# Sigmoid attention and a gated FFN on one core: batch 0 cut into 256 and 192 queries, its loads and FFN runs rearranged, and the first down tile one burst later

## The chip, the cores and the metric

The kernel runs on one core of one Trainium2 chip. The time is the device time of one execution in microseconds (us); medians are over several executions. The profile is of one execution, and its span is some 1.8 us shorter than the device time (429.5 us against 431.3 us for the profiled execution of the kernel before). A program on one core has no second die to compare with, so an execution counts as slow when it is over 1.5% above the fastest of its kernel.

## The reference, cut to what matters

```python
def _attn_ref(q, k, v):                       # (8 batches, 12 heads, 448, 64)
    scores = scale * np.matmul(q, k.transpose(0, 1, 3, 2)) - np.log(S)
    attn = 1.0 / (1.0 + np.exp(-scores))      # a sigmoid: no sum over keys
    return np.matmul(attn, v)

def _moe_ref(x, w_gate, w_val, w_out):        # x: 3584 x 768, hidden 1536
    gate = np.maximum(x @ w_gate, 0.0)
    return (gate * (x @ w_val)) @ w_out
```

Heads of one batch are put side by side to give x. As the attention has no sum over keys, a part of the queries can go all the way through it alone.

## The kernel before

TensorE does five things: scores (`qk_ps`, 64x64 tiles), the product with the values (`pv_ps`, "PV"), a gate and a value product for one of twelve chunks of the hidden layer (`g_ps`, `v_ps`, a "pair"), a down tile (`ya` and `yb`, from the hidden layer with the output weights `wo`), and, for batches 0 and 1, transposes (`trt`). ScalarE does the sigmoids and most rectifiers. VectorE copies transposes, scales PV into xT and multiplies gate and value. GpSimd issues the loads, each of which casts to fp16.

Batch 0 starts from nothing, so it is cut by queries into two halves and runs in six slots (three groups of four heads for each half). A slot has four units: scores, then one sigmoid over up to two chunks of keys. The dictionary `after` says what TensorE is given after each unit. Dummy matmuls (`keep_warm`) fill time.

```python
    QCUT = 3                                  # 3 x 64 = 192 queries first, then 256
    HALVES = ((0, QCUT), (QCUT, NCH))
    ...
    load_gv(0, 2)                             # gate and value weights, chunks 0 and 1
    load(0, 1, NG, "q", QCUT)                 # the rest of batch 0's queries
    load_gv(2, 4)
    load_gv(4, 6)
    load(1, 0, 1, "kq")
    load_gv(6, 9)
    load(1, 1, 2, "kq")
    load_gv(9, 12)
    load_v(1)                                 # the values of batch 1
    load(1, 2, 3, "kq")
    ...
    after = {
        ...                                   # transposes and dummies of the first half
        (3, 0): slots[0].pv,
        (3, 1): two_pv,                       # slots 1 and 2
        (3, 2): lambda: ffn_mix("f"),         # one pair
        (3, 3): second_queries,               # a pair, then transposes
        (4, 1): slots[3].pv,
        (4, 2): lambda: ffn_mix("f"),
        (4, 3): lambda: ffn_mix("f"),
        (5, 1): slots[4].pv,
        (5, 2): lambda: ffn_mix("f"),
        (5, 3): lambda: ffn_mix("f"),
    }
    ...
    def late_loads():                         # near the end of batch 1
        dma_transposes(2, 1)
        hold(2, 1)                            # GpSimd waits here for that transpose
        load_v(2)
        load_o()                              # the output weights wo
    ...
        elif b == 2:                          # "y" is a down tile
            mix = ["ff", "ff", "ffy", "ff", "ffy", "ffy"]
```

From batch 1 on, each batch is six bursts of scores and PVs, each followed by a run of pairs and down tiles of the batch before.

## Time and profile before

| | kernel before |
|---|---|
| device time, median | 431.05 us (430.83 to 431.26, 3 runs) |
| span of the profile | 429.5 us |
| TensorE busy | 418.5 us (97%) |
| ScalarE, VectorE busy | 201.1 us (47%), 141.8 us (33%) |
| TensorE's waits for wo | 1.9 and 1.2 us, at the first down tile |
| loads, 7 to 50 us | about 200 GB/s without a pause |

Read this table from the second row to the last. When one engine is busy 97% of the time, little is gained from making another faster (a stretch in which it only runs dummies counts as busy too, and may be bound by another engine), and what can go is the 3% of holes and any work that is not needed (the dummies). So the holes have to be found one by one, and for each one the question is what ended it.

### The profile page before, as it was taken

To read this page: it belongs to the slowest core of one execution; us is meant where nothing else is said; L and a number is where in the kernel's file an instruction comes from. 1 tells how busy PE (TensorE), PEld (TensorE's weight loads), DVE (VectorE), ACT (ScalarE), POOL (GpSimd) and SP (SyncE) were. 2 spreads that over 40 slices of the span, in tenths; PEclk is the share of its full clock that TensorE was granted. 3 is DMA by queue.
4 is the path that set the end of the run, shared out by engine and by line. 5 is a ranking of instruction groups with operands and counts; after the bars stand their busy time and mean duration, and the time that the engine had idled before them with its cause. 6 is when DMAs were issued, how large, how long until landed. Compare 5 with 4: busy or idle time off the path is not lost.

```text
span 429.5 us, 8576 instructions
## 1 busy us (share of the span) xinstructions
PE 418.5 (97%) x3668; PEld 231.9 (54%) x3668; DVE 141.8 (33%) x277; ACT 201.1 (47%) x424; POOL 49.8 (12%) x73
## 2 busy tenths in 40 slices
PE   8899999889999999999999999999999999999996
PEld 3677774345555455545545455545545554555563
DVE  2453443224233243233242243332442322322231
ACT  5766787434444454446443743473473446122000
POOL 9543204400030001200030000100000000000000
PEclk9999999999999999999999999999999999999999
DMA  9999958999799033951389114721243101100134
GB/s 147 198 202 203 203 81 131 203 220 195 110 155 182 0 81 82 169 104 38 85 122 182 46 43 82 127 56 38 44 88 75 37 2 38 37 2 0 46 102 110
DMA packets 68789, 43.63 MB, mean 102 GB/s; under 512 B 35600, under 2 KB 65168, under 8 KB 68752
## 3 DMA queue, kind: packets, MB, share of 16 engines
q0 software_dynamic: 30736, 23.37, 36.5%
q1 hardware_dynamic: 37664, 19.47, 22.7%
q8 instruction: 28, 0.46, 0.4%
q10 hardware_dynamic: 352, 0.26, 0.2%
q14 instruction: 9, 0.07, 0.1%
HBM read 47.19 MB, written 11.01 MB: 136 GB/s over the span
## 4 chain that ended last, share of the span: by engine, by line
PE 78%; DMA 13%; issue 5%; POOL 3%; DVE 0%; ACT 0%; POOLq 0%
PE g_ps L297 21%; PE v_ps L297 21%; PE ya L335 16%; PE yb L335 9%; PE qk_ps L222 6%; PE pv_ps L240 5%; DMA wo<-in_moe_w_out_dram 4%; DMA v<-in_v_dram 4%; DMA q<-in_q_dram 3%; DMA wg<-in_moe_w_gate_dram 2%; POOL k L97 1%; POOL q L97 1%; POOL v L103 1%; POOL v L101 0%; DVE xT L168 0%
## 5 line engine op out<-in xcount | busy, mean ns | idle before, releaser
L177 ACT ACTIVATE PT<-qk_ps 128x448 f16<-128x448 f32 (+3 forms) x318 | 151.6, 584 | 123.2 <-PE qk_ps L222 122.3
L297 PE MATMUL g_ps<-xT,wg 128*128 128x448 f16 (+2 forms) x648 | 127.5, 333 | 0.2 <-DVE xT L168 0.2
L297 PE MATMUL v_ps<-xT,wv 128*128 128x448 f16 (+2 forms) x648 | 126.8, 332 | 0.3 <-DMA wv<-in_moe_w_val_dram 0.3
L315 DVE TENSOR_TENSOR hT<-gate_sb,v_ps 128x448 f16<-128x448 f32 (+2 forms) x108 | 61.0, 569 | 164.5 <-PE v_ps L297 98.0
L335 PEld LDWEIGHTS <-hT 128*128 128x128 f16 x672 | 65.6, 98 | 50.6 <-DMA wo<-in_moe_w_out_dram 4.0
L297 PEld LDWEIGHTS <-wg 128*128 128x128 f16 x648 | 58.4, 98 | 56.5 <-issue 15.8
L297 PEld LDWEIGHTS <-wv 128*128 128x128 f16 x648 | 62.3, 98 | 47.9 <-DMA wv<-in_moe_w_val_dram 0.6
L306 ACT ACTIVATE gate_sb<-g_ps 128x448 f32<-128x448 f32 (+2 forms) x102 | 54.4, 544 | 70.8 <-PE g_ps L297 70.6
L335 PE MATMUL ya<-wo,hT 128*128 128x512 f16 x336 | 77.1, 379 | 1.9 <-DMA wo<-in_moe_w_out_dram 1.9
L222 PE MATMUL qk_ps<-qkT 64*64 64x448 f16 (+2 forms) x756 | 48.0, 336 | 1.9 <-ACT PT L177 1.1
L335 PE MATMUL yb<-wo,hT 128*128 128x256 f16 x336 | 41.3, 273 | 1.2 <-DMA wo<-in_moe_w_out_dram 1.2
L168 DVE TENSOR_SCALAR xT<-pv_ps 128x448 f16<-128x448 f32 (+2 forms) x54 | 28.4, 568 | 30.8 <-PE pv_ps L240 30.8
L343 DVE TENSOR_SCALAR ysb<-ya 128x512 f32<-128x512 f32 x28 | 19.4, 692 | 56.9 <-PE ya L335 55.0
L240 PE MATMUL pv_ps<-PT,v 64*64 64x448 f16 (+2 forms) x756 | 36.7, 329 | 0.0
L222 PEld LDWEIGHTS <-qkT 64*64 64x64 f16 x756 | 17.8, 105 | 21.6 <-issue 14.3
L240 PEld LDWEIGHTS <-v 64*64 64x64 f16 x756 | 21.6, 107 | 10.8 <-issue 0.5
L101 POOL DMA_DIRECT2D v<-in_v_dram x8 | 6.0, 747 | 174.2 <-PE qk_ps L222 173.9
L343 DVE TENSOR_SCALAR ysb<-yb 128x256 f32<-128x256 f32 x27 | 11.5, 425 | 18.1 <-PE yb L335 18.1
L349 ACT ACTIVATE ysb<-yb 128x256 f32<-128x256 f32 x1 | 0.4, 384 | 27.9 <-PE yb L335 27.9
L97 POOL DMA_DIRECT2D q<-in_q_dram x15 | 11.4, 760 | 8.8 <-PE trt L191 2.9
L97 POOL DMA_DIRECT2D k<-in_k_dram x14 | 10.9, 778 | 7.6 <-DMA wv<-in_moe_w_val_dram 3.5
L103 POOL DMA_DIRECT2D v<-in_v_dram x16 | 10.1, 635 | 2.6 <-DMA wg<-in_moe_w_gate_dram 2.3
(25 smaller groups left out, 59.4 us busy)
## 6 DMA issues: line engine op xcount, KB each, us to landing
out_dram<-ysb SPq DMA_DIRECT2D x54, 192.0 KB, 2.7
k<-in_k_dram POOLq DMA_DIRECT2D x5, 672.0 KB, 13.7
q<-in_q_dram POOLq DMA_DIRECT2D x5, 672.0 KB, 17.0
v<-in_v_dram POOLq DMA_DIRECT2D x8, 336.0 KB, 5.3
v<-in_v_dram POOLq DMA_DIRECT2D x16, 168.0 KB, 6.6
k<-in_k_dram POOLq DMA_DIRECT2D x8, 224.0 KB, 10.4
wo<-in_moe_w_out_dram POOLq DMA_DIRECT2D x1, 1536.0 KB, 15.4
q<-in_q_dram POOLq DMA_DIRECT2D x6, 224.0 KB, 11.2
```

The lines of the kernel that those rows point to most:

```text
L97: nc.gpsimd.dma_start(t16[:, xs, cs], rows_of(src, b)[:, xs, cs])
L101: nc.gpsimd.dma_start(v16[:, 0::2, :], rows_of(v, b)[:, 0::2, :])
L103: nc.gpsimd.dma_start(v16[64 - 64 * r : P - 64 * r, 1::2, :], rows_of(v, b)[64 * r : 64 * r + 64, 1::2, :])
L168: nc.vector.tensor_scalar(out=xT_of(b, pr)[:, q0 : q0 + qn], in0=src, scalar1=XSCALE, scalar2=None, op0=AOP.mult,)
L177: nc.scalar.activation(PT_ap, ps_ap, AF.Sigmoid, bias=sig_bias, scale=qk_scale)
L222: nc.tensor.matmul(out_of(hh)[o : o + 64, :], qkT[rows, c, cols], qkT[rows, NCH + c0 : NCH + c1, cols], start=True, stop=True, tile_positi ...
L240: nc.tensor.matmul(ps[hh][64 * r : 64 * r + 64, 0:qn], v16[rows, 2 * g + hh, c * D : (c + 1) * D], pieces[c][rows, hh, :], start=(c == 0), ...
L297: nc.tensor.matmul(ps[-1][:, 0:qn], wt[:, dc, f * P : (f + 1) * P], xT_tiles[(b, dc)][:, q0 : q0 + qn], start=(dc == 0), stop=(dc == NDC - 1),
L306: nc.scalar.activation(gate_sb[:, 0:qn], ps[0][:, 0:qn], AF.Relu)
L315: nc.vector.tensor_tensor(out=hT_tiles[(g, f)][:, o : o + qn], in0=gate_sb[:, 0:qn], in1=ps[1][:, 0:qn], op=AOP.mult,)
L335: nc.tensor.matmul(ps[:, 0 : m1 - m0], hT_tiles[(g, f)][:, t * P : (t + 1) * P], wo[:, f, m0:m1], start=(f == 0), stop=(f == NFC - 1),)
L343: nc.vector.tensor_scalar(out=ysb[:, m0:m1], in0=ps[:, 0 : m1 - m0], scalar1=OUT_SCALE, scalar2=None, op0=AOP.mult)
```

## The change

It has four parts. Batch 0's first half grows to 256 queries and its second shrinks to 192. The rest of the queries is loaded between the first gate weights and the first value weights. The PVs of the first half move into the stretch that the sigmoids bound, and the pairs stand in fewer, longer runs, which saves changes of TensorE's tiling. And the first down tile of batch 2 stands one burst later, when wo has landed.

```diff
-    QCUT = 3
+    QCUT = 4
...
-    load_gv(0, 2)
+    load_gv(0, 2, (0,))
     load(0, 1, NG, "q", QCUT)
+    load_gv(0, 2, (1,))
     load_gv(2, 4)
...
     def second_queries():
-        ffn_mix("f")
         for g in range(1, NG):
             pe_transposes(0, g, 1, QCUT, NCH)
-    def two_pv():
-        slots[1].pv()
-        slots[2].pv()
+    def pv_then_ffn(i):
+        slots[i].pv()
+        ffn_mix("f")
...
-        (3, 0): slots[0].pv,
-        (3, 1): two_pv,
-        (3, 2): lambda: ffn_mix("f"),
-        (3, 3): second_queries,
-        (4, 1): slots[3].pv,
-        (4, 2): lambda: ffn_mix("f"),
-        (4, 3): lambda: ffn_mix("f"),
-        (5, 1): slots[4].pv,
-        (5, 2): lambda: ffn_mix("f"),
+        (2, 2): slots[0].pv,
+        (2, 3): slots[1].pv,
+        (3, 1): slots[2].pv,
+        (3, 2): second_queries,
+        (3, 3): lambda: ffn_mix("f"),
+        (4, 1): lambda: pv_then_ffn(3),
+        (4, 3): lambda: ffn_mix("ff"),
+        (5, 1): lambda: pv_then_ffn(4),
         (5, 3): lambda: ffn_mix("f"),
...
-            mix = ["ff", "ff", "ffy", "ff", "ffy", "ffy"]
+            mix = ["ff", "ff", "ff", "ffy", "ffy", "ffy"]
```

More of the change, by code (lines that the diff above doesn't have):

```diff
@@ L129, with load_gv @@
     wo = wpool.tile([P, NFC, DM], FP16, name="wo")
-    def load_gv(f0, f1):
+    def load_gv(f0, f1, which=(0, 1)):
         fs = slice(f0 * P, f1 * P)
-        nc.gpsimd.dma_start(wg[:, :, fs], moe_w_gate[:, fs].rearrange("(c p) f -> p c f", p=P))
-        nc.gpsimd.dma_start(wv[:, :, fs], moe_w_val[:, fs].rearrange("(c p) f -> p c f", p=P))
-    load_gv(0, 2)
+        for i in which:
+            wt, src = ((wg, moe_w_gate), (wv, moe_w_val))[i]
+            nc.gpsimd.dma_start(wt[:, :, fs], src[:, fs].rearrange("(c p) f -> p c f", p=P))
+    load_gv(0, 2, (0,))
     load(0, 1, NG, "q", QCUT)
+    load_gv(0, 2, (1,))
     load_gv(2, 4)
```

## The prediction

> **What bounds the kernel now.** I read the page's busy line first, then the list of what TensorE waited for, then the timeline of TensorE and ScalarE over the first 110 us, then the landing time of each load.
>
> ```profile
> PE 418.5 (97%) x3668; PEld 231.9 (54%) x3668; DVE 141.8 (33%) x277; ACT 201.1 (47%) x424; POOL 49.8 (12%) x73
> ...
> PE ya L335 <- DMA wo<-in_moe_w_out_dram: 1.9, 1, 1.9
> PE yb L335 <- DMA wo<-in_moe_w_out_dram: 1.2, 1, 1.2
> ```
>
> TensorE is busy 97% of 429.5 us and no engine comes near it, so the end is set by TensorE's work plus the holes in it. The list of waits shows just two holes above 1 us after the start-up, both at the first down tile, both for the output weights wo. The timeline shows their cost:
>
> ```profile
> 82.04 1.30 PE L297 MATMUL v_ps<-xT,wv 128*128 128x448 f16 x6
> 85.25 2.76 PE L335 MATMUL ya<-wo,hT 128*128 128x512 f16 x12 [1.91 <-DMA wo<-in_moe_w_out_dram]
> 89.22 1.48 PE L335 MATMUL yb<-wo,hT 128*128 128x256 f16 x12 [1.20 <-DMA wo<-in_moe_w_out_dram]
> 90.63 0.76 PE L222 MATMUL qk_ps<-qkT 64*64 64x448 f16 x12
> ...
> 102.73 2.75 PE L335 MATMUL ya<-wo,hT 128*128 128x512 f16 x12
> 105.32 1.47 PE L335 MATMUL yb<-wo,hT 128*128 128x256 f16 x12
> 106.72 0.76 PE L222 MATMUL qk_ps<-qkT 64*64 64x448 f16 x12
> ```
>
> An undisturbed tile takes 106.72 - 102.73 = 3.99 us. The first could have begun when the six value matmuls before it had gone out, at 82.04 + 1.14 = 83.18 (1.14 is the start-to-start of such a run elsewhere), and have ended at 87.17. It ended at 90.63, so the real loss is 3.46 us, a little over the 3.1 us of listed waits.
>
> The start is the other place. ScalarE's timeline:
>
> ```profile
> 6.36 2.77 ACT L177 ACTIVATE PT<-qk_ps 128x768 f16<-128x768 f32 x4 [1.34 <-PE qk_ps L222]
> 9.78 5.51 ACT L177 ACTIVATE PT<-qk_ps 128x768 f16<-128x768 f32 x8 [0.65 <-PE qk_ps L222]
> 15.65 1.94 ACT L177 ACTIVATE PT<-qk_ps 128x1024 f16<-128x1024 f32 x2 [0.36 <-PE pv_ps L240]
> ...
> 21.99 3.56 ACT L177 ACTIVATE PT<-qk_ps 128x1024 f16<-128x1024 f32 x4 [1.78 <-PE qk_ps L222]
> ```
>
> From 6.4 to 15.3 ScalarE runs nearly without a gap: the three first-half slots (192 queries each) are bound by the sigmoids, and TensorE fills its time with dummy matmuls. From 15.3 to 31 it is the other way round: ScalarE has gaps, and TensorE does real work almost all the time (second-half scores, all six PV products, six gate/value pairs).
>
> **What the skill says.** "TensorE: Matmul & The Clock Gate", section "Wait — 56ns, not 53.3ns?", gives N/2.4 GHz plus 2.5 ns for a warm matmul: 109 ns at 256 columns and 82.5 ns at 192. The trace agrees: runs of six take 0.655 and 0.495 us start to start. So a pair costs 1.31 us at 256 queries and 0.99 at 192, in proportion to queries, and swapping the halves leaves TensorE's total alone. "TensorEngine Tiling (Array Packing)", section "Key Properties", says that a change of tiling mode drains the array; here, going from a 128x128 run to a 64x64 one costs 0.09 us (94.74 to 95.97 is 1.23 us, not 1.14). "ScalarE: Activation LUTs", section "What ACT_TABLE_LOAD costs", gives 186 ns + 0.833 ns per element; the 128x1024 sigmoid (1023 ns) and the 128x768 one (810 ns) are near it. "DMA: Bandwidth & Descriptors", "Specifications", wants runs of 512 B or more. The change makes each group's early query rows 512 B (384 B before) and its late rows 384 B (512 B before), so by the end of batch 0 the mix is the same. The loads run at about 200 GB/s from 7 to 50 us, well below that page's limits, but that is what this mix gives.
>
> **The change, part by part.**
>
> *The down tile a burst later* (batch 2's list of runs). Its 3.99 us of work moves behind three scores (0.70) and one run of two pairs (4.55). It would then begin at 83.27 + 5.25 = 88.52 and need the second half of wo at 91.1. wo landed at 69.84 + 15.4 = 85.2 and 70.90 + 18.27 = 89.17. Both are in time, by 3.3 and 1.9 us, so the whole 3.46 us goes. The margin bears the start-up becoming 1 us shorter too.
>
> *256 queries first.* A slot's sigmoids take 3.5 us (last ScalarE row above), not 2.77. The first query load is 256 KB instead of 192, and its cast 128 elements longer; I allow 0.35 us. First sigmoid at 6.7, then 3 x 3.5: first half done at 17.2 instead of 15.3. The 0.65 us gap vanishes, because group 1's copy (ready at 9.3, say 9.7 now) is before the 10.2 at which it is wanted. That is 1.9 us lost, but PV 0 and 1 now lie inside it, and PV 2 just after it. They cost 0.61 us each after the first slots before; at 256 queries 0.89.
>
> My walk of TensorE afterwards, with rows of the timeline before: batch 0's values land at 7.25 + 7.9 = 15.15 before, some 0.4 us later now (64 KB more through the same queue, 64 KB more in the first load, at 200 GB/s). PV 0 at 15.6 to 16.5, PV 1 to 17.55, two scores, PV 2 17.9 to 18.8, one score, twelve transposes (0.5), one score, and the first pair at 19.8 when xT is copied. The rest of the queries now lands about 18, since 384 KB of value weights no longer go before it; the value weights land at 18.5 + 1.3 = 19.8 (256 KB more ahead of them) and are wanted at 20.45, so the 0.29 us wait there goes. Then five more pairs at 1.31, two PVs at 0.65, the scores: fourth to sixth slot done at about 31.3. Before, the same point (the transposes of batch 1) is at 31.13.
>
> So the clock there is 0.2 us later, but six pairs have been done at 256 queries, not 192: 6 x 0.32 = 1.9 us less is left. Net 1.7 us ahead. One run of pairs fewer (five for six) is in this: about 0.1 us.
>
> *What is kept of it.* The 1.9 us comes back in the next six pairs (192 queries now), before batch 1's first PV product. That product is here:
>
> ```profile
> 48.40 1.49 PE L240 MATMUL pv_ps<-PT,v 64*64 64x448 f16 x28
> ...
> 33.33 0.63 POOL L103 DMA_DIRECT2D v<-in_v_dram  x1 [2.26 <-DMA wg<-in_moe_w_gate_dram]
> ...
> v<-in_v_dram POOLq DMA_DIRECT2D x1, 168.0 KB, 14.2
> ```
>
> The rows are TensorE's first PV of batch 1, the issue of the last piece of that batch's values, and its time from issue to landing. It lands at 33.33 + 14.2 = 47.53, 0.87 us before it is used. The queue is full from the start and the bytes ahead of this piece are the same in both kernels, so I expect it at 47.5 again. TensorE will be ready at 48.4 - 1.7 = 46.7 and will wait 0.8 us, for the values and for nothing else: a new wait in place of work. What is left of the 1.7 us is 0.87.
>
> Sum: 3.46 + 0.87 = 4.33 us; 431.05 - 4.33 = 426.7 us, 1.0% less. After the first down tile each batch has the same runs as before, and TensorE's work in them is unchanged, so I carry the gain to the end undiminished. Batch 3's keys and queries land at 92.5 and 96.6; the copies that need them would come at about 94.7 instead of 99, so VectorE may wait until 96. The products that it owes TensorE next are due at 96.3, so I count nothing for it.
>
> **Rivals.** (1) *The values of batch 1 do not hold it up*, because larger early loads fill the slow first 7 us of DMA (109 and 138 GB/s in its slices, against 200 later) and all lands earlier: gain 5.2 us, 425.9. Against it: only 128 KB are brought forward, worth at most 0.6 us. (2) *The first half costs more than I think*: ScalarE gaps whenever a PV sits between two scores, or batch 0's values land late with nothing else to do. Were the start-up 1 us slower than the walk, 0.7 us would be left and the wait at the batch 1 values would shrink instead: 0.2 us worse, 426.9. Only a start-up 2 us slower would lose the early gain whole and more: 427.9. So the wait for those values makes the result insensitive to the start. (3) *The down tile meets wo late again*, if the output weights are issued later or share the queue with batch 3's loads for longer. They are released by the transposes of batch 2, which move with TensorE, 0.2 to 0.9 us earlier. A second half landing at 91.5 would cost 0.5 us. (4) *ScalarE becomes the bound in batch 1's first bursts*, where three sigmoid units now stand against three pairs of 0.99 us. Six sigmoids take 2.72 us and three rectifiers 1.0; TensorE takes 3.8: just even, so at most some tenths before the same wait.
>
> **Range and chances.** The 3.46 us is read straight from the trace and hardly doubtful; the early part I put between -0.4 and +1.6. That gives 427.9 to 425.9 and, with the run-to-run spread of 0.2 us, a range of 425.6 to 428.0. Two per cent is 8.6 us, twice all that I can find, and a loss of that size would need several microseconds of new waits: faster 0.03, within 0.96, slower 0.01.
>
> **What will show it.** Right: no wait of TensorE for wo; first sigmoid near 6.7 and the first 128x1024 run of twelve units ending near 17.2; batch 1's first transposes near 31.3; a wait of TensorE (or of its weight loads) of about 0.8 us for batch 1's values, with its first PV near 47.6; 4.3 us of lead at the first tile's end and the same lead at the end. Wrong: first PV of batch 1 before 47 (then rival 1), transposes after 32.3 (rival 2), a wo wait (rival 3), or a lead that shrinks after 100 us, which would mean that a later load has become the limit.

## The result, and the profile after

The changed kernel took 427.04 us (median of 4 runs, 426.36 to 427.39); the kernel before, run beside it, 430.97 us. The ratio is 0.9906, with a 95% interval of 0.9889 to 0.9923. A ratio in this document is the mean time of one kernel's fast runs over that of the other's in the same rounds, so it is not quite the ratio of the medians quoted. The span went from 429.5 to 425.2 us.

First, all that TensorE waited for in the changed kernel (columns: total us, times, longest):

```profile
PE warm_ps L162 <- DVE zeros L116: 1.2, 1, 1.2
PE qk_ps L224 <- DVE qkT L198: 0.5, 1, 0.5
PE pv_ps L242 <- issue: 0.5, 1, 0.5
PE g_ps L299 <- DVE xT L170: 0.2, 1, 0.2
```

Neither wait for wo is left, and the wait for the first value weights is gone too. There is no wait for batch 1's values. But there is one line that the list of before did not have: 0.5 us inside a PV product that has "issue" as its releaser, that is, nothing that the profile shows.

The first down tile, in TensorE's timeline (start, length, what; no bracket at the end means no idle time before it):

```profile
86.53 1.30 PE L299 MATMUL v_ps<-xT,wv 128*128 128x448 f16 x6
87.66 2.75 PE L337 MATMUL ya<-wo,hT 128*128 128x512 f16 x12
90.25 1.47 PE L337 MATMUL yb<-wo,hT 128*128 128x256 f16 x12
91.66 0.57 PE L224 MATMUL qk_ps<-qkT 64*64 64x448 f16 x8
```

The tile follows its pairs at once and takes 91.66 - 87.66 = 4.00 us. The second tile ends at 102.41 here and at 106.72 before, so the lead is 4.31 us there, and it is 429.5 - 425.2 = 4.3 us at the end: nothing is lost on the way.

ScalarE's sigmoids in batch 0:

```profile
7.46 3.35 ACT L179 ACTIVATE PT<-qk_ps 128x1024 f16<-128x1024 f32 x4 [2.26 <-PE qk_ps L224]
11.09 9.37 ACT L179 ACTIVATE PT<-qk_ps 128x1024 f16<-128x1024 f32 x12 [0.28 <-PE qk_ps L224]
21.62 1.51 ACT L179 ACTIVATE PT<-qk_ps 128x768 f16<-128x768 f32 x2 [1.17 <-PE qk_ps L224]
```

The second row is twelve units without a gap: two slots of the first half and the first of the second (the timeline names only the first shape of a run). ScalarE works without a gap until 20.46; the last sigmoid of the first half ends at 17.80. So this stretch is bound by ScalarE, with the first three PVs beside it (on TensorE at 15.74, 16.61 and 18.01). The first sigmoid is 1.1 us later than before (7.46 against 6.36).

And TensorE's fourth PV product:

```profile
21.50 0.67 PE L242 MATMUL pv_ps<-PT,v 64*64 64x192 f16 x23
22.62 0.32 PE L242 MATMUL pv_ps<-PT,v 64*64 64x192 f16 x5 [0.45 <-issue]
...
32.32 0.58 PE L193 MATMUL trt<-ident,k 128*64 128x128 f16 x14
...
47.67 1.49 PE L242 MATMUL pv_ps<-PT,v 64*64 64x448 f16 x28
```

The product stops after 23 of its 28 matmuls. Batch 1's transposes begin at 32.32 (31.13 before), and its first PV at 47.67 (48.40 before), so the start-up gives a lead of 0.73 us, less than its last load allowed: the values' last piece was issued at 32.59 and took 14.2 us, so it landed at 46.79.

### The profile page after: what moved, and what is told of

Same layout as the page of the kernel before. It is cut to its first block, busy times and chain, and to the rows that moved or that the text cites. A ratio compares the mean times of both kernels' runs of the same rounds, so it can differ in the third digit from the quotient of the medians.

```text
span 425.2 us, 8576 instructions
## 1 busy us (share of the span) xinstructions
PE 418.5 (98%) x3668; PEld 232.8 (55%) x3668; DVE 142.2 (33%) x277; ACT 200.1 (47%) x424; POOL 49.4 (12%) x73
## 4 chain that ended last, share of the span: by engine, by line
PE 96%; ACT 2%; DVE 1%; issue 0%
PE g_ps L299 27%; PE v_ps L299 26%; PE ya L337 17%; PE yb L337 9%; PE qk_ps L224 9%; PE pv_ps L242 7%; ACT PT L179 2%; PE warm_ps L162 1%; PE trt L193 1%; DVE xT L170 0%; DVE qkT L198 0%; ACT ysb L351 0%; DVE zeros L116 0%
## 5 line engine op out<-in xcount | busy, mean ns | idle before, releaser
L170 DVE TENSOR_SCALAR xT<-pv_ps 128x448 f16<-128x448 f32 (+2 forms) x54 | 28.4, 568 | 30.4 <-PE pv_ps L242 30.3
L224 PEld LDWEIGHTS <-qkT 64*64 64x64 f16 x756 | 17.8, 106 | 20.1 <-issue 12.5
L345 DVE TENSOR_SCALAR ysb<-yb 128x256 f32<-128x256 f32 x27 | 11.5, 425 | 16.7 <-PE yb L337 16.7
## 6 DMA issues: line engine op xcount, KB each, us to landing
wo<-in_moe_w_out_dram POOLq DMA_DIRECT2D x1, 1536.0 KB, 13.2
```

The costliest lines, as they stand in the source:

```text
L170: nc.vector.tensor_scalar(out=xT_of(b, pr)[:, q0 : q0 + qn], in0=src, scalar1=XSCALE, scalar2=None, op0=AOP.mult,)
L224: nc.tensor.matmul(out_of(hh)[o : o + 64, :], qkT[rows, c, cols], qkT[rows, NCH + c0 : NCH + c1, cols], start=True, stop=True, tile_positi ...
L345: nc.vector.tensor_scalar(out=ysb[:, m0:m1], in0=ps[:, 0 : m1 - m0], scalar1=OUT_SCALE, scalar2=None, op0=AOP.mult)
```

## The experiments

Twelve kernels ran, all with correct results, in three sets, each with runs of the kernel before on the same chip (medians 431.18 us for the first set, 431.10 for the other two). Each was timed in five rounds; the medians are of 4 to 6 runs of it. My theory was: the down tile gives about 3.5 us, and the start-up about 0.9, which is what the values of batch 1 leave of a larger lead. The rivals were that the larger half costs more than I thought, that the values land earlier, and that the pause seen above is what holds the start-up back. I had no run in which the places of the PVs and the grouping of the pairs are changed apart from each other.

**The changed kernel once more** (`after_again`; no edit).

> The changed kernel once more, for its spread and for a second profile. Theory: about 427.0 us. In the first profile the array ran its first matmuls slowly until about 7 us (first sigmoid at 7.46 instead of the predicted 6.7) and TensorE paused 0.45 us inside the fourth PV product with no releaser shown. If these are accidents of one execution, this profile shows one or both absent (first sigmoid near 6.8, no pause) and the times spread by about 1 us; if they belong to the kernel, both are there again.

Measured: 426.96 us (426.63 to 427.26), ratio 0.9903 (0.9888 to 0.9918). The first sigmoid came at 6.95, so its late start was partly an accident of one execution. The pause was there again, at the same matmul, for 0.45 us, so it belongs to the kernel. Batch 1's transposes began at 31.81 and its first PV at 47.16, just before the last values (issued 33.06, 14.3 us, so 47.36): the product was stretched by about 0.25 us (the next transposes have a lead of only 0.27 us over the first execution, where the earlier ones had 0.51).

**The down tile alone** (`tile_only`, on the kernel before).

```diff
-            mix = ["ff", "ff", "ffy", "ff", "ffy", "ffy"]
+            mix = ["ff", "ff", "ff", "ffy", "ffy", "ffy"]
```

> Only the later first down tile, on the kernel before. Theory: no wait for wo at all, 3.46 us gained, 427.6 us. Rival: only the 3.1 us of listed waits or less comes back because batch 3's loads become the limit: 428 us or more.

Measured: 428.10 us (427.59 to 428.28), ratio 0.9926 (0.9913 to 0.9938). Its tile in TensorE's timeline:

```profile
88.77 2.75 PE L335 MATMUL ya<-wo,hT 128*128 128x512 f16 x12
91.36 1.47 PE L335 MATMUL yb<-wo,hT 128*128 128x256 f16 x12
92.77 0.57 PE L222 MATMUL qk_ps<-qkT 64*64 64x448 f16 x8
```

There is no wait. This execution was 0.26 us behind the profiled one of the kernel before at batch 1's transposes (31.39 against 31.13), and 3.21 us ahead at the second tile (99.52 + 3.99 = 103.51 against 106.72): together 3.47 us, what the loss was reckoned at. The median gain is 431.18 - 428.10 = 3.1 us; the 0.4 us between is within the spread of the start-up. The time itself is the one that the rival named (428 or more), but its reason is not there: TensorE waits for no load of batch 3, and the lead of 3.21 us is 429.5 - 426.2 = 3.3 us at the end.

**The start-up alone** (`start_only`: the changed kernel, with the first down tile put back).

```diff
-            mix = ["ff", "ff", "ff", "ffy", "ffy", "ffy"]
+            mix = ["ff", "ff", "ffy", "ff", "ffy", "ffy"]
```

> The whole start-up of the change with the first down tile where it was. If the two parts simply add, it gains what the full change has over the tile alone, 0.5 to 0.9 us: 430.1 to 430.5. Theory: the wait for wo hides the lead or adds to it according to when wo lands; in the profile of the changed kernel its second half landed at 88.0 (89.2 before), so 429.9 to 430.2 with a wait for wo of 3 us or more still there. Rival: wo's landing does not move, the lead is eaten whole: 431.0.

Measured: 430.63 us (430.23 to 430.82), ratio 0.9983 (0.9971 to 0.9996). That is less of a gain than either of my sums said (429.9 to 430.2, or 430.1 to 430.5), though not the rival's 431.0. Two places of TensorE's timeline carry the reading:

```profile
47.20 0.45 PE L242 MATMUL pv_ps<-PT,v 64*64 64x448 f16 x3
48.06 1.51 PE L242 MATMUL pv_ps<-PT,v 64*64 64x448 f16 x25 [0.42 <-DMA v<-in_v_dram]
...
84.59 2.76 PE L337 MATMUL ya<-wo,hT 128*128 128x512 f16 x12 [1.61 <-DMA wo<-in_moe_w_out_dram]
88.55 1.48 PE L337 MATMUL yb<-wo,hT 128*128 128x256 f16 x12 [1.20 <-DMA wo<-in_moe_w_out_dram]
```

The predicted wait for batch 1's values is in this execution: the product stopped after three matmuls until they landed (32.74 + 15.3 = 48.04). And as long as the tile meets wo, a lead in front of it is worth only as much as wo itself lands earlier: 88.55 here, 89.22 before. So the two parts are worth 0.55 us and 3.1 us alone, and 4.2 together (431.18 - 426.96).

**The loads as before** (`loads_back`).

```diff
-    load_gv(0, 2, (0,))
+    load_gv(0, 2)
     load(0, 1, NG, "q", QCUT)
-    load_gv(0, 2, (1,))
```

> The changed kernel with the gate and value weights loaded together again, the rest of the queries behind both. Theory: the late queries then land near 19 us and are wanted at 19.1, so 0 to 0.3 us slower than the change, no more (427.0 to 427.3). Rival: the load order is what makes the rearranged slots possible: a wait of TensorE of over 1 us at the second transposes of the queries, 428 us or more.

Measured: 427.40 us (427.16 to 429.03), ratio 0.9918 (0.9903 to 0.9933); its profile has a wait of 0.5 us of the transposes for the queries. A little more than the 0 to 0.3 us expected: the load order is worth some 0.4 us, though the interval overlaps that of the change.

**wo loaded early, tile in its old place** (`wo_early`, on the kernel before).

```diff
         hold(2, 1)
         load_v(2)
-        load_o()
...
                     load(2, 2, 3, "kq")
+                    load_o()
```

> The kernel before, tile order untouched, but the output weights issued at the first run of batch 1 instead of after the transposes of batch 2. They should land before 75 us, long before the tile at 83.2. Theory: the whole cost there was the wait, so the tile's place does not matter: as tile_only, 427.6 to 428.1. Rival: the order of the work matters too, or the early 2.25 MB push other loads into a wait: 429 us or more.

Measured: 436.98 us (436.34 to 437.56), ratio 1.0135 (1.0121 to 1.0148). The rival held, and by more than it said:

```profile
70.65 0.96 PE L222 MATMUL qk_ps<-qkT 64*64 64x448 f16 x8 [5.96 <-DMA qkT<-rel]
...
74.91 2.06 PE L297 MATMUL g_ps<-xT,wg 128*128 128x448 f16 x6
...
92.39 2.75 PE L335 MATMUL ya<-wo,hT 128*128 128x512 f16 x12
```

The tile had no wait. But the 2.25 MB of wo, issued at 50.3, were now under way together with batch 2's transposes by DMA, which took 12.6 us instead of 5.0 (medians of issue to landing, 50 to 75 us), and the scores of batch 2 stood still for 6 us. After this gap TensorE's granted clock read 0.50 from 72 to 76 us, and six gate matmuls took 1.9 us start to start instead of 1.14. So loading wo this early is no way round the wait. Whether the tile's old place would have been as good with wo at hand, this run cannot tell, as the new wait hides it.

**256 queries first, PVs and pairs in their old places** (`cut4_old_slots`: `after` and its helpers from the kernel before, all else changed).

> The change (256 queries first, its loads, its tile) with the old places of the PV products and pairs. Theory: the larger first half alone costs, as the sigmoids run 2 us longer with TensorE idle or on dummies and the three PVs (0.89 each) come after it: transposes of batch 1 at 33.5 or later instead of 32, 428.2 to 429.0. Rival: the places of the PVs do not matter, the size does all: 427.0.

Measured: 428.87 us (428.37 to 429.01), ratio 0.9944 (0.9932 to 0.9956), as expected. TensorE waits for sigmoids, the PVs come after them, and batch 1's transposes begin at 34.38:

```profile
16.45 0.30 PE L224 MATMUL qk_ps<-qkT 64*64 64x256 f16 x4 [0.50 <-ACT PT L179]
17.36 0.36 PE L224 MATMUL qk_ps<-qkT 64*64 64x192 f16 x8 [0.61 <-ACT PT L179]
17.53 0.96 PE L242 MATMUL pv_ps<-PT,v 64*64 64x256 f16 x28
...
34.38 0.58 PE L193 MATMUL trt<-ident,k 128*64 128x128 f16 x14
```

**192 queries first, PVs and pairs in their new places** (`slots_cut3`).

```diff
-    QCUT = 4
+    QCUT = 3
```

> The change with 192 queries first again, but the new places of the PVs and pairs. Theory: the first PV then comes at about 13 us, before batch 0's values land (13.9 to 15.2), so TensorE waits 1 to 2 us for them and the sigmoids behind it stand still; as the pairs are small again nothing pays for that: 428 to 429. Rival: the places of the PVs do all the work and 256 queries none: 427.0.

Measured: 428.44 us (427.98 to 429.25), ratio 0.9940 (0.9927 to 0.9953). The time is as expected but not for the reason given: the first PV began at 14.49, with no wait for values, and TensorE had two pauses with no releaser (0.58 and 0.84 us), again after 23 of 28 matmuls of a PV product:

```profile
16.46 0.32 PE L242 MATMUL pv_ps<-PT,v 64*64 64x192 f16 x5 [0.58 <-issue]
...
22.65 0.38 PE L242 MATMUL pv_ps<-PT,v 64*64 64x256 f16 x5 [0.84 <-issue]
```

Set beside `tile_only`, which has neither, these two are the most useful of the runs:

| | old places | new places |
|---|---|---|
| 192 first | 428.10 (`tile_only`) | 428.44 |
| 256 first | 428.87 | 426.96 |

The larger half alone loses 0.8 us, the new places alone change nothing that can be told from the spread (0.3 us slower), and both together win 1.1 us. The intervals of the ratios overlap a little in all three cases; the single times overlap only in the second. (`tile_only` also has the old loads; in `loads_back` those were worth 0.4 us.) More queries in the first half make the sigmoids' stretch longer, which costs as long as TensorE has only dummies to do in it; the PVs in that stretch are the work that fills it. By the traces that accounts for a part of the 2.06 us by which the transposes of `cut4_old_slots` come after those of the change (34.38 against 32.32): its first pair begins 0.65 us later (20.38 against 19.73). The rest lies behind the first pair, where the old places also have the transposes of the late queries, 0.85 us with the wait for their copy, more changes of tiling, and two waits of 0.23 us for sigmoids. How much is due to the PVs and how much to the grouping of the pairs, no run separates. With 192 queries the new places lose visibly in the two pauses, 1.4 us together; where they come from, the run `shifted` helps to tell. I have no run with 192 queries and no pauses.

**The values of batch 1 later** (`v1_late`).

```diff
-    load_v(1)
     load(1, 2, 3, "kq")
+    load_v(1)
```

> The changed kernel with batch 1's values loaded behind its last keys and queries (0.45 MB, 2.2 us at 200 GB/s). Theory: the values land near 49.4 and TensorE, ready at 47.2 to 47.7, waits some 2 us at batch 1's first PV; nothing later gives it back: 428.8 to 429.2. Rival: there was slack behind it (the later waits absorb it): 427.0 to 427.5.

Measured: 429.24 us (429.06 to 431.23), ratio 0.9963 (0.9947 to 0.9979), 2.3 us more than the change. Batch 1's first PV:

```profile
48.23 0.35 PE L242 MATMUL pv_ps<-PT,v 64*64 64x448 f16 x2
48.98 0.37 PE L242 MATMUL pv_ps<-PT,v 64*64 64x448 f16 x1 [0.39 <-DMA v<-in_v_dram]
49.87 1.51 PE L242 MATMUL pv_ps<-PT,v 64*64 64x448 f16 x25 [0.52 <-DMA v<-in_v_dram]
```

Its bulk starts at 49.87, and batch 1's last transposes at 54.41, 2.2 to 2.5 us later than in the two executions of the change (52.20 and 51.93). The loss goes through to the end. So the landing of these values is a wall for the start-up, and the change stands within a microsecond of it, on either side: they landed 0.9 us before the first PV began in the first execution of the change and 0.8 us after it in `start_only`. (The second stop is also before TensorE's instruction number 1472, which is 704 + 3 x 256, a place of the kind that the run `shifted` below finds. It is still the values: the instruction packet for it began 9 us earlier, at 40.80, and in `v1_early` and the first execution of the change TensorE passes the same instruction without a stop.)

**The values of batch 1 earlier** (`v1_early`).

```diff
-    load_gv(9, 12)
     load_v(1)
+    load_gv(9, 12)
     load(1, 2, 3, "kq")
```

> The changed kernel with batch 1's values loaded before the last gate and value weights (landing near 42 us). In the profiles so far TensorE reached batch 1's first PV 0.2 to 0.4 us before they landed in three executions of the new start-up of four. Theory: the wait is gone, 0 to 0.4 us gained: 426.6 to 426.9. Rival: the last weights, 0.67 MB later, become late themselves: a wait at the pair that needs them near 50 us, 427.3 or more.

Measured: 426.58 us (426.43 to 427.19), ratio 0.9899 (0.9884 to 0.9913). The values landed at 42.2 and no wait took their place. It is the lowest median of all, 0.4 us below the change and as expected, but the intervals overlap, so I call it the same. Its first PV of batch 1:

```profile
47.17 1.49 PE L242 MATMUL pv_ps<-PT,v 64*64 64x448 f16 x28
```

It begins no earlier than in `after_again` (47.16), but runs without a stretch: with the wall gone, the start-up up to this point is no faster.

**The instructions shifted** (`shifted`).

```diff
-        (1, 3): lambda: keep_warm(2),
-        (2, 0): lambda: keep_warm(2),
+        (1, 3): lambda: nudge(14),       # 14 matmuls of 32 columns
+        (2, 0): lambda: nudge(14),
```

> The changed kernel with four wide dummy matmuls in the first half replaced by 28 narrow ones, so 48 more TensorE instructions before the second half. Theory: the 0.4 to 0.7 us pause after the 23rd matmul of the fourth PV product is TensorE's instruction stream running dry (each 16 KB instruction packet is 256 instructions; the one before the pause began 2 us earlier). It then falls elsewhere, in a slower stretch, and is gone; batch 1's transposes come 0.4 to 0.7 us earlier than in the change, near 31.2, and the values of batch 1 take most of it: 426.6 to 427.0. Rival: the pause belongs to that product's own waits and stays where it is: 427.0 or slower.

Measured: 427.57 us (426.82 to 427.94), ratio 0.9913 (0.9898 to 0.9928). I was wrong that the pause would be gone (the transposes came at 33.12, not near 31.2), and by the time alone the rival would have won; but the pause did not stay with its product, and where it went says what it is:

```profile
16.73 0.27 PE L247 MATMUL pv_ps<-PT,v 64*64 64x256 f16 x1 [0.44 <-issue]
...
22.92 0.24 PE L229 MATMUL qk_ps<-qkT 64*64 64x192 f16 x1 [1.03 <-issue]
```

The pause of the change was before the 24th matmul of its fourth PV. In the list of TensorE's instructions of the built program (numbered from its initial branch) that is instruction 704; the trace agrees, as it is the 352nd matmul and each has its weight load. With 48 instructions more in front, the pause stands before the last score matmul ahead of that product, and that one is now number 704:

```
change:   702 Matmult pv_ps<-PT,v 64x192    703 Ldweights    704 Matmult pv_ps<-PT,v 64x192
shifted:  702 Matmult qk_ps<-qkT 64x192     703 Ldweights    704 Matmult qk_ps<-qkT 64x192
```

The other pause of `shifted` is before number 448, which is 704 - 256. The two of `slots_cut3` are also before 448 and 704. The trace has instruction packets of 16 KB on a DMA queue of their own, 28 of them in this kernel (0.46 MB). One of them starts in the slice of 20.1 to 20.2 us of the changed kernel:

```profile
q8 instruction: 1, 0.02, 55.8%
```

By the trace's records it starts at 20.12, and the pause ends at 22.62, 2.50 us later. In `after_again` it is 19.59 and 22.10; in `start_only` 19.69 and 22.14; in `shifted` 20.47 and 22.92. Over all twelve listed pauses of the nine runs that have one it is 2.35 to 2.57 us. So it looks as if TensorE stands still when it reaches such an instruction before about 2.5 us have passed since the packet was begun. This is not a sharp limit: `v1_late` passed number 448 after 2.24 us and `pv_earlier` number 704 after 2.43 us without a listed pause. The link is inferred from the place in the list, the 256 between places and the nearly constant delay; no view shows the fetch itself. In the profile of the kernel before, that packet began at 19.10 and number 704, the 12th matmul of its fourth PV, came at 22.16, 3.1 us later: no pause. But its start-up is at the edge too: in `tile_only` and `wo_early`, which have it unchanged, this same matmul starts 0.21 and 0.30 us after the one before it instead of 0.003, 2.4 us after the packet began. So the change did not bring this pause in; it made it longer.

**The PVs earlier still** (`pv_earlier`).

```diff
-        (2, 0): lambda: keep_warm(2),
+        (2, 0): slots[0].pv,
...
-        (2, 2): slots[0].pv,
-        (2, 3): slots[1].pv,
+        (2, 2): slots[1].pv,
+        (3, 0): second_queries,
         (3, 1): slots[2].pv,
-        (3, 2): second_queries,
```

> The changed kernel with the first PV product in place of two dummy matmuls after the first unit of slot 3, the second where the first was, and the late queries' transposes one unit earlier. Theory: batch 0's values have landed (13.9), the first pair starts 0 to 0.8 us earlier (not before the value weights at 19.0), and then the values of batch 1 stop it: 426.5 to 427.0. Rival: the extra product delays the sigmoids that bind this stretch: 427.3 or more.

Measured: 426.89 us (426.57 to 427.23), ratio 0.9901 (0.9888 to 0.9914): the same as the change. The first PV waited 0.6 us for batch 0's values, the sigmoids behind it got a gap of 0.87 us, and in exchange no pause is listed: its packet began at 19.96 and number 704 was reached at 22.39. One loss was traded for another.

**All three together** (`combined`: the edits of `v1_early` and `pv_earlier`, and the narrow dummies at the places (1, 0) and (1, 3)).

> All three: the PVs earlier, the instructions shifted, the values of batch 1 before the last weights. If the waits hide behind each other, none alone gives much and all together do: batch 1's transposes near 30.6, its first PV near 46, no wait, 425.3 to 426.0. Rival: the later transposes, copies and the output weights (landing 88) hold the first down tile: 426.5 to 427.

Measured: 427.22 us (427.02 to 427.84), ratio 0.9911 (0.9898 to 0.9924). Two pauses, of 0.27 and 0.81 us, were back, the second before instruction 704 (packet at 20.14, pause ended at 22.64), probably because the narrow dummies use up instructions fast; transposes began at 32.79, not near 30.6. Neither of my two theories for this run is right: the start-up was late before any later load could hold it. From one matmul's start to the next, the two pauses take 0.54 and 1.06 us of these 2.2 us; the rest was not traced. No version beat the change beyond the spread.

## Why the prediction was right or wrong

The time was right: 426.7 predicted, 427.04 and 426.96 measured, inside the range of 425.6 to 428.0. That the start-up's share came out is in part luck, as its steps show.

**The down tile** was right in cause and size. It was put at 3.46 us; the profiles of `tile_only` and of the kernel before show 3.47, and the times 3.1. With the predicted lead, the tile was to start at 88.52 - 0.87 = 87.65; it started at 87.66. wo landed about 1.1 us earlier than in the kernel before (70.87 + 13.2 = 84.1 for its first part, 85.2 before), though it was issued 1.0 us later; so the reason I gave against the third rival, that its release moves with TensorE, failed, and the conclusion held. Why wo then took 13.2 us and not 15.4 was not tested.

**The start-up** was right in total and wrong in three of its steps. It was to give 0.87 us; the profile shows 0.73 at batch 1's first PV, and the times 431.18 - 426.96 - 3.08 = 1.1 us on top of the tile.

- The step "transposes of batch 1 at about 31.3" failed: 32.32 and 31.81 in the two executions. Two things were missing. One is the pause in the fourth PV: that product took 22.87 - 21.50 = 1.37 us, and the fifth 0.68, so the pause cost about 0.7 us. The other is in the sum behind the first pair. I allowed 31.3 - 19.8 = 11.5 us; without the pause it took 32.32 - 19.73 - 0.7 = 11.9. The terms that I named come to less still, about 30.4 with the scores at the 1.5 us that the trace has: I named two PVs of the second half where there are three (0.7 us each), and no change of tiling after the five runs of pairs (0.1 us each).
- The walk up to the first pair matched the first profile (19.8 predicted, 19.73 measured), but two errors offset each other in it. I had the first PV wait for batch 0's values at 15.5; they landed at about 14.0 (issued at 7.2), and why they were earlier was not tested. And the first sigmoid, put at 6.7, came at 7.46, so the first half's sigmoids ended at 17.80 and not at 17.2 (0.28 us of the gap in front of the second slot stayed), and the first PV, at 15.74, waited for its turn behind the sigmoids. In `start_only` the first sigmoid came at 6.73 as predicted, and there the first pair began at 19.00, 0.8 us ahead of the walk. The first sigmoid (6.95 in `after_again`) scatters with the execution, and between the two executions of the change its 0.51 us are still there at the transposes. Where it was late, TensorE's first matmuls were slow for longer: the two dummies before the first scores took 0.93 us in the change's profile and also in `tile_only`, whose start is the same as before, but 0.55 in `start_only`, in `after_again` and in the kernel before.
- The step "lands at 47.53 in both kernels, TensorE will wait 0.8 us" was right about the wall and wrong in its size. The values landed at 46.79 and 47.36 in the two profiles of the change and at 48.04 in `start_only`, and TensorE was there at 47.67, 47.16 and 47.20, not at 46.7: a wait of none, about 0.25, and 0.8 us (from one matmul's start to the next). `v1_late` shows that the wall is real, `v1_early` that little is lost to it. So my first and second rivals were each half true: the start-up was 0.5 to 1 us slower than the walk, and because it was, the values held it up little or not at all. I had written that a slower start would only shrink that wait, and had put 426.9 on it; that is why the total held. But the cause that I gave there, gaps of ScalarE or late values of batch 0, is not the one found.

**No new bound** came after 100 us, as said: the lead was 4.31 us at the second tile and 4.3 us at the end.

## What to carry to other kernels

When TensorE is the bound, list its waits and read each one's true loss from the same work elsewhere in the trace; moving work behind a transfer that is late is then worth what that difference says, and it kept its value to the end here, while loading the data earlier put the transfer in the way of others and lost 6 us. A stretch bound by another engine and the work that could fill it have to be changed together: here the longer stretch alone lost 0.8 us, the moved work alone won nothing, and both won 1.1 us. And where two walls stand close behind each other, do not add up the gains in front of them.

## What the Trainium skill lacked or had wrong

- "Runtime: NRT & Kernel Launch", section "Instruction fetch mechanics", says that instructions come in 16 KiB blocks of 256 and that the fetch is hidden because the sequencer issues slower than the blocks arrive. The size agrees (28 packets of 16 KB, pauses 256 instructions apart). Hidden it was not: with the load queue full, TensorE stood still for 0.27 to 1.2 us before instruction 448 or 704 in nine of the ten runs that have the new places of the PVs, and went on 2.35 to 2.57 us after the packet began. That the fetch is the cause is inferred from these places and this delay. Runs of 64x64 matmuls use up 56 instructions in 0.7 us.
- "DMA: Bandwidth & Descriptors": no section gives a figure for how much longer a DMA transpose takes beside plain loads on another queue. In `wo_early` it went from 5.0 to 12.6 us (medians) beside 2.25 MB of loads.
